# A pre-LN attention and SwiGLU block: where the feed-forward weights are summed and split

## The chip, the core and the metric

The kernel runs on one core of a Trainium2 chip. Five engines work side by side, each through its own instructions in order: TensorE (PE; its weight loads are listed as PEld), VectorE (DVE), ScalarE (ACT), GpSimd (POOL) and SyncE (SP), which issues nearly all DMA transfers here. They meet only at semaphores. The metric is device time of one execution in microseconds (us); lower is better.

## The reference

One transformer block on 2048 tokens of width 640, 32 heads of 20, a feed-forward width of 1728, all in f32:

```
x = A_x
h = x + attention(layernorm(x), A_wqkv, A_wo)       # softmax(q k^T / sqrt(20)) v, then @ wo
z = layernorm(h)
out = h + (silu(z @ w_gate) * (z @ w_up)) @ w_down
```

## The kernel before

**Precision.** Most products are made from a high part, rounded to the fast matmul format (fp32r), and a low part, the rest: `split` writes the high part on ScalarE (line 74) and the low one by a subtraction on another engine (line 75). A product of two split operands is three matmuls: high x high, high x low, low x high.

**Stages.** (1) Normalisation, q, k, v and a part of the row maxima, up to about 370 us. (2) Attention, to about 1545 us: 32 units (8 groups of four heads, 4 chunks of 512 queries) of 16 key tiles. One step is one key tile: four score matmuls (`scores`, line 796), four exponentials on ScalarE (802), four weighted sums of an earlier step (`weigh`, 806), and row maxima for later units (`max_one`, 175 and 181) spread by `ORDER`. When a unit's maxima are complete, `max_all` (line 185) reduces them on VectorE and copies and splits them on GpSimd (`both`, 192 and 193); two steps later `max_finish` transposes them on TensorE (200), copies them on ScalarE (202), and SP writes them into rows of the query tile by four transfers (207). After a unit, its sums go through DRAM to be spread over partitions (819, 829, 835), GpSimd multiplies (841) and SP stores (844). (3) The projection of the last chunks, to about 1590 us. (4) The feed-forward stage, to the end.

**The feed-forward stage.** The 1728 columns of gate and up are cut into 14 blocks (the last of 64 columns), and the 2048 tokens into two pairs of chunks. `elements` is the list of (pair, block), the half block first in each pair. Gate and up of a block are computed together by a scheme of seven products (`UNITS`: A11, S2, A12, S1, S3, A22, S4, made from sums and differences of quarters of the weights and of the tokens) and four products with the last 128 rows (K4). `blocks` runs the products, `plain` those of the half block. One product is one step (8 a block, 6 in the half block), and after each, `step` issues what belongs beside it: some of the 16 pieces of the product with `w_down` of the block before (`down`, line 1026 on TensorE and the addition 1031 on VectorE), and preparations. Accumulators are four banks `ps_a` for products and four `ps_b` for `down`.

**Weights before the change.** `Weights` (669) loads a block's raw columns on SP (678), lets GpSimd make the four sums (704 to 711), and splits seven units of 128 x 256 and the last rows on ScalarE and GpSimd (`unit`, `last`, through 74 and 75) into a ring of 8 unit tiles and one of 3 last tiles. `load_down` and `split_down` do the same for 128 rows of `w_down`. Each block is prepared during the block before, and so each is loaded, summed and split twice, once a pair. Only the half block and the first whole one are made within attention, by GpSimd alone (`weights_ahead`, 718 and 719), from step (NU - NC) * NT + 5 = 453 of 512 on.

**The second pair's tokens.** `late_tokens` (1156) normalises, transposes, splits and sums chunks 2 and 3 while the first pair runs: 15 small items (`soon`), then 21 (`late`) of which four token tiles take five each: two flips (five transposes, copies and splits), sums on GpSimd, two splits. Results go to DRAM (`z_d`, `t_d`) from the tiles `kept`, of which each shape has two buffers. `soon` is taken one a step from step 3 of the first whole block on, `late` one every third step. During the last block of the first pair and the half block of the second, `swap` (1236) loads them back over the first pair's tiles.

Of the kernel before, what the change touches and what calls it, by code (L numbers as in the profile page):

```python
# [43 lines left out]
def tile_block(ctx: ExitStack, tc: tile.TileContext, x, wqkv, wo, wg, wu, wd, out):  # L44
# [11 lines left out]
    t_d = [dram.tile([P, 2, 4, CH], F32R, name=f"t_d{i}") for i in range(2)]  # L56

# [600 lines left out]
    rings = {}  # L658

    def place(kind):  # L660

        if not rings:
            rings["unit"] = [stay.tile([P, 8, 2, 2, P], F32R, name="units", tag="first"), 8, 0]
            rings["last"] = [stay.tile([P, 3, 2, 2, P], F32R, name="lasts", tag="second"), 3, 0]
        ring = rings[kind]
        ring[2] += 1
        return ring[0][:, (ring[2] - 1) % ring[1]]

    class Weights:


        def __init__(self, f):
            self.f, self.units, self.ahead = f, {}, False

        def load_one(self, i):
            f, src = self.f, (wg, wu)[i]
            cs = slice(f * P, (f + 1) * P)
            nc.sync.dma_start(self.raw[i], src[:, cs].rearrange("(k p) n -> p k n", p=P))

        def load(self):  # L680
            f = self.f
            both = pd1.tile([P, 2, ND, P], F32, name="raw")
            self.raw = [both[:, 0], both[:, 1]]
            self.ends = both[:, :, ND - 1]
            if f < NF - 1:
                for i in range(2):
                    self.load_one(i)
            else:
                self.load_half()

        def load_half(self):
            for i, src in enumerate((wg, wu)):
                nc.sync.dma_start(
                    self.raw[0][:, :, i * LASTW : (i + 1) * LASTW],
                    src[:, self.f * P :].rearrange("(k p) n -> p k n", p=P),
                )

        def sums(self, part, pool, tag):
            g, u = self.raw
            t = pool.tile([P, 2, 2, P], F32, name="sums", tag=tag, bufs=2)  # L700
            tt = nc.gpsimd.tensor_tensor
            a, b = t[:, 0], t[:, 1]
            if part == 0:
                tt(out=a, in0=u[:, 0:2], in1=u[:, 2:4], op=ALU.add)
                tt(out=b, in0=a, in1=g[:, 0:2], op=ALU.subtract)
                self.sources = {
                    "A11": g[:, 0:2], "A12": g[:, 2:4], "A22": u[:, 2:4], "S1": a, "S2": b,
                }
            else:
                tt(out=a, in0=g[:, 0:2], in1=u[:, 0:2], op=ALU.subtract)  # L710
                tt(out=b, in0=g[:, 2:4], in1=self.sources["S2"], op=ALU.subtract)
                self.sources.update({"S3": a, "S4": b})

        def part(self, src, hi, lo):
            if not self.ahead:
                split(src, hi, lo, nc.gpsimd)
                return
            nc.gpsimd.tensor_copy(hi, src)
            nc.gpsimd.tensor_tensor(out=lo, in0=src, in1=hi.bitcast(F32), op=ALU.subtract)

        def unit(self, kind, where="unit"):
            if self.f == NF - 1:
                k = 0 if kind == "A11" else 2
                src = self.raw[0][:, k : k + 2]
            else:
                src = self.sources[kind]
            t = self.units[kind] = place(where)
            self.part(src, t[:, 0], t[:, 1])

        def last(self):  # L730
            t = self.units["K4"] = place("last")
            n = 2 if self.f < NF - 1 else 1
            if self.ahead:
                for i in range(n):
                    self.part(self.raw[i][:, ND - 1], t[:, 0, i], t[:, 1, i])
            else:
                self.part(self.ends[:, :n], t[:, 0, :n], t[:, 1, :n])

        def tasks(self):

            u = self.unit
            if self.f == NF - 1:
                return [
                    [self.load], [], [lambda: u("A11")], [lambda: u("A12")], [self.last],
                ]
            return [
                [self.load], [],
                [lambda: self.sums(0, pd1, "sums"), lambda: u("A11")],
                [lambda: self.sums(1, pd1, "sums"), lambda: u("S2")],
                [lambda: u("A12"), self.last], [lambda: u("S1")],  # L750
                [lambda: u("S3"), lambda: u("A22")], [lambda: u("S4")],
            ]

        def raw_tile(self):
            return pc.tile([P, ND, P], F32, name="raw", tag="o_t")

    def weights_ahead():

        half, whole = Weights(NF - 1), Weights(0)
        half.ahead = whole.ahead = True  # L760

        def load_half():
            half.raw = [half.raw_tile()]
            half.load_half()

        def load(i):
            if i == 0:
                whole.raw = []
            whole.raw.append(whole.raw_tile())
            whole.load_one(i)  # L770

        nothing = lambda: None

        def half_first():
            keep = rings["unit"][2]
            rings["unit"][2] = 7
            half.unit("A11")
            rings["unit"][2] = keep

        tasks = [load_half, lambda: load(0), nothing, half.last]  # L780
        tasks += [lambda: half.unit("A12", "last"), half_first, lambda: load(1), nothing, nothing]
        tasks += [lambda: whole.sums(0, pc, "z2"), lambda: whole.sums(1, pc, "z2")]
        tasks += [lambda k=k: whole.unit(k) for k in UNITS] + [whole.last]
        return half, whole, tasks
# [86 lines left out]
    half_block, first_block, preparing = weights_ahead()  # L871
    for u in range(NU):
# [4 lines left out]
        for kt in range(NT):  # L877
# [45 lines left out]
            if kt in (12, 13) and 0 <= k + kt - 12 < ND:  # L923
                load_wo(k + kt - 12)
# [67 lines left out]
    def load_down(f):  # L992
        raw = pd2.tile([P, D], F32, name="d_raw")
        if f < NF - 1:
            nc.sync.dma_start(raw, wd[f * P : (f + 1) * P, :])
        else:
            for i in range(2):
                nc.sync.dma_start(raw[i * LASTW : (i + 1) * LASTW, :], wd[f * P :, :])
        return raw

    def split_down(raw):
        hi = pd2.tile([P, D], F32R, name="d_hi", bufs=2)
        lo = pd2.tile([P, D], F32R, name="d_lo", bufs=2)
        split(raw, hi, lo, nc.gpsimd)
        return hi, lo

# [10 lines left out]
    def down(c, t, half, wts, y_hi, y_lo, final):  # L1017
        d_hi, d_lo = wts
        tt = c * TPC + t
        pairs = [(y_hi, d_hi), (y_hi, d_lo)]  # L1020
        if y_lo is not None:
            pairs.append((y_lo, d_hi))
        hs = slice(half * HALF, (half + 1) * HALF)
        ps = ps_b()
        for n, (a, b) in enumerate(pairs):
            nc.tensor.matmul(  # L1026
                ps[:, :HALF], a[:, t * P : (t + 1) * P], b[:, hs],
# [9 lines left out]
    def to_come(c, wts, y, final):  # L1037
        pending.extend(
            lambda t=t, half=half: down(c, t, half, wts, *y, final)
            for t in range(TPC) for half in range(2)  # L1040
        )
# [11 lines left out]
    def plain(w, step, done):  # L1053

        u = w.units
        for i, order in enumerate(("124", "142")):
            z, ps = z2_c[i], bank()
            for n, k in enumerate(order):
# [7 lines left out]
                if n == 2:  # L1066
                    done(i, gated(ps))
                step()

    def blocks(w, step, done):  # L1070

        u = w.units
        z0, z1 = z2_c[0], z2_c[1]
        add = lambda out, ps, x: nc.vector.tensor_tensor(out=out, in0=ps, in1=x, op=ALU.add)  # L1074
# [6 lines left out]
        products(ps, two_of(u["S2"]), two_of(t32, 2))  # L1081
# [3 lines left out]
        products(ps, two_of(u["A12"]), two_of(z0, 2), True, False)  # L1085
# [5 lines left out]
        products(ps, two_of(u["S1"]), two_of(t14))  # L1091
# [228 lines left out]
```

## Time and profile before

| what | value |
|---|---|
| median of 3 runs | 2134.91 us (2133.05 to 2136.81) |
| the profiled execution, its own time | 2131.16 us |
| its span in the profile | 2129.2 us |
| TensorE busy, of the span | 98% |
| VectorE / ScalarE / GpSimd busy | 83% / 64% / 28% |
| granted TensorE clock | 0.998 |
| DMA, mean | 81 GB/s |

In the rows below, "out<-in xcount" names a group of instructions by the tiles it writes and reads; "| busy, mean ns | idle <-releaser" gives its total time in us, the mean of one instruction in ns, and how long the engine stood idle right before these instructions, with what ended the wait. A timeline row is start and length in us, and in brackets the idle time before it. A windows row is start:end and length in us, then each engine's busy us with its instructions, the granted clock, the busy share of the 16 DMA engines, and GB/s. Matmuls overlap, so their mean is longer than their spacing. A row of DMA in the chain of waits is a transfer from its issue to its landing. `SPq` rows are the issue of transfers by SP.

### The profile page before, as it was taken

The numbers are of one execution on the slowest core, as the hardware profiler recorded it, in microseconds if no ns is written. First come the engines' busy times: TensorE is split into PE (matmuls) and PEld (weight loads), VectorE is DVE, ScalarE is ACT, GpSimd is POOL, SyncE is SP. The second block draws the span as 40 slices with busy tenths as digits, with TensorE's granted clock in tenths as the row PEclk, the third lists the DMA queues.
The fourth block names the chain that finished last, engine by engine and source line by source line (L and its number), as shares of the span: only waits on it lengthen the run. The fifth ranks groups of instructions, "written<-read, shape, count | busy, mean of one in ns | idle before, by whom it ended". The sixth has DMA issues, their size and how long they took to land.

```text
span 2129.2 us, 34742 instructions
## 1 busy us (share of the span) xinstructions
PE 2094.9 (98%) x12726; PEld 1222.6 (57%) x12726; DVE 1761.4 (83%) x2929; ACT 1358.6 (64%) x2722; POOL 586.3 (28%) x644
## 2 busy tenths in 40 slices
PE   7999999999999999999999999999999999999999
PEld 5766775333333333333333333345588888888888
DVE  6999996999999999999999999986368776666666
ACT  4222217999998999989998999986733433233322
POOL 5222212000000000000000011031147888576664
PEclk9999999999999999999999999999999999999999
DMA  7565432110211211102103122121132343732111
GB/s 243 185 178 174 153 108 82 56 52 19 78 29 41 66 37 56 47 24 63 44 20 80 27 60 78 41 68 35 51 102 75 107 120 89 220 107 56 44 56 68
DMA packets 165009, 172.42 MB, mean 81 GB/s; under 512 B 41112, under 2 KB 109208, under 8 KB 164840
## 3 DMA queue, kind: packets, MB, share of 16 engines
q1 hardware_dynamic: 151256, 143.99, 23.1%
q10 hardware_dynamic: 13584, 26.23, 4.0%
q8 instruction: 100, 1.64, 0.3%
q14 instruction: 69, 0.57, 0.1%
HBM read 121.93 MB, written 47.45 MB: 80 GB/s over the span
## 4 chain that ended last, share of the span: by engine, by line
PE 88%; DVE 5%; DMA 3%; POOL 1%; issue 1%; SPq 1%; ACT 1%; ACTq 0%; POOLq 0%; DVEq 0%
PE acc L806 24%; PE ps_max L175 15%; PE ps_one L796 14%; PE ps_a L956 14%; PE ps_b L1026 8%; PE ps_one L416 4%; DVE mx L169 3%; PE ps_one L450 2%; PE ps_wide L165 2%; PE ps_max L606 2%; PE ps_b L606 1%; DMA qk_d<-e 1%; DMA raw<-in_B_w_up 1%; DVE mx L181 1%; DMA o_t<-o_d 0%
## 5 line engine op out<-in xcount | busy, mean ns | idle before, releaser
L802 ACT ACTIVATE probs<-ps_one 128x512 f32<-128x512 f32 x2048 | 1045.0, 623 | 133.7 <-PE ps_one L796 128.3
L181 DVE TENSOR_REDUCE mx<-ps_max 128x1 f32<-128x512 f32 x1632 | 1021.2, 683 | 97.6 <-PE ps_max L175 50.1
L796 PE MATMUL ps_one<-q_stk,k_stk 62*128 62x512 f32 x2048 | 551.8, 422 | 1.8 <-DMA h<-in_A_x 1.1
L806 PE MATMUL acc<-probs,v_stk 128*32 128x512 f32 x4096 | 546.3, 605 | 0.2
L175 PE MATMUL ps_max<-k_stk,q_stk 60*128 60x512 f32 x1632 | 542.3, 460 | 2.2 <-DVE mx L181 1.5
L175 PEld LDWEIGHTS ps_max<-k_stk,q_stk 60*128 60x128 f32 x1632 | 231.1, 184 | 428.9 <-DVE mx L181 410.0
L796 PEld LDWEIGHTS ps_one<-q_stk,k_stk 62*128 62x128 f32 x2048 | 300.1, 186 | 82.0 <-ACT probs L802 52.7
L169 DVE TENSOR_REDUCE mx<-ps_wide 128x2 f32<-128x1024 f32 x208 | 240.5, 1216 | 13.2 <-PE ps_wide L165 12.6
L1074 DVE TENSOR_TENSOR tmp<-ps_a,tmp 128x512 f32<-128x512 f32 x208 | 141.2, 690 | 132.6 <-PE ps_a L956 126.6
L192 POOL CAST both<-neg 128x16 fp32r<-128x16 f32 x32 | 6.6, 206 | 788.3 <-DVE neg L188 396.7
L1031 DVE TENSOR_TENSOR h<-ps_b,h 128x320 f32<-128x320 f32 x448 | 197.2, 482 | 13.2 <-PE ps_b L1026 13.0
L806 PEld LDWEIGHTS acc<-probs,v_stk 128*32 128x32 f32 x4096 | 80.8, 108 | 160.9 <-issue 152.6
L956 PE MATMUL ps_a<-t,units 128*128 128x512 f32 x624 | 162.7, 396 | 0.0
L1026 PE MATMUL ps_b<-d_hi,y_hi 128*128 128x320 f32 x448 | 138.6, 310 | 0.7 <-DVE h L1031 0.7
L1026 PE MATMUL ps_b<-d_lo,y_hi 128*128 128x320 f32 x448 | 137.7, 308 | 1.1 <-POOL d_lo L75 1.1
L74 ACT ACTIVATE y_hi<-tmp 128x512 fp32r<-128x512 f32 (+1 forms) x56 | 35.3, 632 | 161.9 <-DVE tmp L1075 156.9
L956 PE MATMUL ps_a<-z,units 128*128 128x512 f32 x504 | 130.9, 394 | 0.0
L1026 PE MATMUL ps_b<-d_hi,y_lo 128*128 128x320 f32 x416 | 127.6, 307 | 3.0 <-POOL y_lo L75 3.0
L956 PEld LDWEIGHTS ps_a<-t,units 128*128 128x128 f32 x624 | 112.6, 188 | 18.7
L956 PEld LDWEIGHTS ps_a<-z,units 128*128 128x128 f32 x504 | 90.8, 187 | 15.3
L1088 ACT ACTIVATE tmp<-tmp 128x512 f32<-128x512 f32 x26 | 16.5, 633 | 126.4 <-DVE tmp L1074 126.4
L956 PE MATMUL ps_a<-z,lasts 128*128 128x512 f32 x336 | 95.3, 393 | 0.0
(152 smaller groups left out, 2181.4 us busy)
## 6 DMA issues: line engine op xcount, KB each, us to landing
raw<-qk_d SPq DMA_DIRECT2D x70, 160.0 KB
k_stk<-qk_d SPq DMA_DIRECT2D x64, 160.0 KB
q_stk<-qk_d SPq DMA_DIRECT2D x64, 160.0 KB
raw<-in_B_w_gate SPq DMA_DIRECT2D x26, 320.0 KB
raw<-in_B_w_up SPq DMA_DIRECT2D x26, 320.0 KB
d_raw<-in_B_w_down SPq DMA_DIRECT2D x26, 320.0 KB
rb<-r_d SPq DMA_DIRECT2D x32, 256.0 KB
qk_d<-e ACTq DMA_DIRECT2D x22, 320.0 KB
```

Of the source, the lines that this page charges most:

```text
L169: nc.vector.tensor_reduce(mx[:, :, pair, t, kc], ps, axis=AX.X, op=ALU.max)
L175: nc.tensor.matmul(ps, queries[u][rows, pair, t * P : (t + 1) * P], keys[u // NC][rows, pair, kc * CH : (kc + 1) * CH], start=True, stop=True,
L181: nc.vector.tensor_reduce(mxs[u][:, b, pair, t, kc : kc + 1], ps, axis=AX.X, op=ALU.max)
L416: nc.tensor.matmul(ps, w[:, k, m * P : (m + 1) * P], a[:, k, :], start=(n == 0 and k == 0), stop=(n == 2 and k == ND - 1),)
L606: nc.tensor.matmul(ps[:, :HALF], a[:, k, :], w[:, k, hs], start=(n == 0), stop=(n == 3 * ND - 1),)
L796: nc.tensor.matmul(ps, keys[u // NC][rows, p, kt * P : (kt + 1) * P], queries[u][rows, p, :], start=True, stop=True,)
L802: nc.scalar.activation(probs[p][:, b, :], ps, AF.Exp, scale=scale)
L806: nc.tensor.matmul(acc[32 * j : 32 * j + 32, :], values[u // NC][:, kt, j * VW : j * VW + 32], probs[j // 2][:, j % 2, :], start=(kt == 0) ...
L956: nc.tensor.matmul(ps, w[k][:, i], z[k][:, j], start=(first and m == 0), stop=(last and m == len(n) - 1),)
L1026: nc.tensor.matmul(ps[:, :HALF], a[:, t * P : (t + 1) * P], b[:, hs], start=(n == 0), stop=(n == len(pairs) - 1),)
L1031: nc.vector.tensor_tensor(out=h, in0=ps[:, :HALF], in1=h, op=ALU.add)
L1074: add = lambda out, ps, x: nc.vector.tensor_tensor(out=out, in0=ps, in1=x, op=ALU.add)
```

## The change

All feed-forward weights are prepared once, within attention, on GpSimd alone, and written to DRAM (`w_d`: per block eight places of 128 x 512, seven units and the last rows; `d_d`: per block two half rows of `w_down`, high and low). `prepare_weights` gives a list of 204 tasks: for each whole block load, a pause, two pairs of sums, seven units and the last rows; for the half block load, pause, two units and the last rows; for `w_down`, of two blocks at a time, load, pause and four half rows. Each task first issues the stores of the task before. Raw weights use the tiles `o_t`, sums `z2`, results `o_hi` and `o_lo`, two buffers each, which nothing else uses at that time. From unit 1 on, each step takes one task, but for key tiles 3 and 4 and for the step in which `max_all` was just issued.

The last stage no longer sums or splits weights. Three rings of tiles are filled by SP from DRAM, a unit, a last or a half row at a time: `Ring.fill` is called at the start of each step and issues loads into places that had been freed at the call before. The rings of 8 units and 3 lasts are first filled at step (NU - NC) * NT + 8, that of 4 half rows when the projection is done. Also, `soon` is now taken five a step from the first step on, `late` one every step, and the pieces of `down` beside the first whole block are spread as 0, 0, 3, 3, 3, 3, 2, 2.

```diff
+    w_d = [dram.tile([P, 8, 4 * P], F32R, name=f"w_d{f}") for f in range(NF)]
+    d_d = [dram.tile([P, 2, 2 * HALF], F32R, name=f"d_d{f}") for f in range(NF)]
...
-    class Weights:
...
-    def weights_ahead():
...
+    def prepare_weights():
+        stores, count = [], [0]
+        def store():
+            while stores:
+                dst, t = stores.pop(0)
+                nc.sync.dma_start(dst.bitcast(F32), t.bitcast(F32))
+        def staged(shape):
+            count[0] += 1
+            return pc.tile(shape, F32R, name="staged", tag=("o_hi", "o_lo")[count[0] % 2])
+        def part(src, hi, lo):
             nc.gpsimd.tensor_copy(hi, src)
             nc.gpsimd.tensor_tensor(out=lo, in0=src, in1=hi.bitcast(F32), op=ALU.subtract)
...
+            def unit(kind):
+                store()
+                t = staged([P, 2, 2, P])
+                part(src[kind], t[:, 0], t[:, 1])
+                stores.append((w_d[f][:, UNITS.index(kind)], t.rearrange("p i k n -> p (i k n)")))
...
+    class Ring:
+        def __init__(self, places, plan):
+            self.places, self.plan = places, plan
+            self.issued = self.taken = self.freed = self.before = 0
+        def fill(self):
+            while self.issued < min(len(self.plan), self.before + len(self.places)):
+                place = self.places[self.issued % len(self.places)]
+                dst, src = self.plan[self.issued](place)
+                nc.sync.dma_start(dst.bitcast(F32), src.bitcast(F32))
+                self.issued += 1
+            self.before = self.freed
...
                 max_all(a[0])
+                quiet[0] = now[0]
...
-                    if preparing and now[0] >= (NU - NC) * NT + 5:
+                    if preparing and u and kt not in (3, 4) and quiet[0] != now[0]:
                         preparing.pop(0)()
+                    if now[0] == (NU - NC) * NT + 8:
+                        unit_ring, last_ring = weight_rings()
+                        unit_ring.fill()
+                        last_ring.fill()
...
-    def load_down(f):
...
-    def split_down(raw):
...
+        def by_unit(ps, *args):
+            products(ps, two_of(unit_ring.take()), *args)
+            unit_ring.free()
...
-        products(ps, two_of(u["A11"]), two_of(z0))
+        by_unit(ps, two_of(z0))
...
+    halves = pd2.tile([P, 4, 2, HALF], F32R, name="halves")
+    down_ring = Ring(
...
+    down_ring.fill()
...
-            each = [0, 0, 0, 3, 3, 3, 3, 4]
+            each = [0, 0, 3, 3, 3, 3, 2, 2]
...
-            for t in tasks[n]:
-                t()
-            if n == 3:
-                dn["parts"] = split_down(dn["raw"])
+            for ring in (unit_ring, last_ring, down_ring):
+                ring.fill()
...
-            if soon and (e > 1 or n >= 3):
-                soon.pop(0)()
-            elif late and not soon and count[0] % 3 == 0:
+            if soon:
+                for _ in range(5):
+                    if soon:
+                        soon.pop(0)()
+            elif late:
                 late.pop(0)()
```

More of the change, by code (lines that the diff above doesn't have):

```diff
@@ L657, in tile_block @@
     UNITS = ("A11", "S2", "A12", "S1", "S3", "A22", "S4")
[L658 to L667, printed above, removed]
-    class Weights:
[L672 to L717, printed above, removed]
@@ L730, in last @@
[L730 to L752, printed above, removed]
@@ L754, in raw_tile, with nothing @@
-        def raw_tile(self):
-            return pc.tile([P, ND, P], F32, name="raw", tag="o_t")
-    def weights_ahead():
[L759 to L784, printed above, removed]
+        def nothing():
+            store()
@@ new lines, in rows, with load, half @@
+        def rows(fs):
+            raw = {}
+            def load():
+                store()
+                for f in fs:
+                    raw[f] = pc.tile([P, D], F32, name="raw", tag="o_t")
+                    if f < NF - 1:
+                        nc.sync.dma_start(raw[f], wd[f * P : (f + 1) * P, :])
+                    else:
+                        for i in range(2):
+                            nc.sync.dma_start(
+                                raw[f][i * LASTW : (i + 1) * LASTW, :], wd[f * P :, :]
+                            )
+            def half(f, i):
+                store()
+                t = staged([P, 2, HALF])
+                part(raw[f][:, i * HALF : (i + 1) * HALF], t[:, 0], t[:, 1])
+                stores.append((d_d[f][:, i], t.rearrange("p i n -> p (i n)")))
+            return [load, nothing] + [lambda f=f, i=i: half(f, i) for f in fs for i in range(2)]
@@ new lines, in prepare_weights, with take, free @@
+        tasks = []
+        for f in range(NF):
+            tasks += block(f)
+        for f in range(0, NF, 2):
+            tasks += rows((f, f + 1))
+        return tasks + [store]
+    class Ring:
[9 more added lines that the diff above has]
+            self.before = self.freed
+        def take(self):
+            assert self.taken < self.issued
+            self.taken += 1
+            return self.places[(self.taken - 1) % len(self.places)]
+        def free(self, n=1):
+            self.freed += n
@@ new lines, in tile_block, with weight_rings, unit, last @@
+    ELEMENTS = [(pair, f) for pair in range(2) for f in (NF - 1, *range(NF - 1))]
+    def weight_rings():
+        def unit(f, i):
+            return lambda t: (t.rearrange("p i k n -> p (i k n)"), w_d[f][:, i])
+        def last(f):
+            n = 2 if f < NF - 1 else 1
+            return lambda t: (
+                t[:, :, :n], w_d[f][:, 7].rearrange("p (i k n) -> p i k n", i=2, k=2)[:, :, :n]
+            )
+        units = stay.tile([P, 8, 2, 2, P], F32R, name="units", tag="first")
+        lasts = stay.tile([P, 3, 2, 2, P], F32R, name="lasts", tag="second")
+        plan = [
+            unit(f, i) for _, f in ELEMENTS for i in (range(7) if f < NF - 1 else (0, 2))
+        ]
+        return (
+            Ring([units[:, i] for i in range(8)], plan),
+            Ring([lasts[:, i] for i in range(3)], [last(f) for _, f in ELEMENTS]),
+        )
@@ L990, in quarter_sums @@
         ]
-    def load_down(f):
[L993 to L999, printed above, removed]
-    def split_down(raw):
[L1002 to L1005, printed above, removed]
     def parts(f, s):
@@ L1015, in parts, with down @@
         return y_hi, None
-    def down(c, t, half, wts, y_hi, y_lo, final):
-        d_hi, d_lo = wts
+    def down(c, t, half, d, y_hi, y_lo, final):
         tt = c * TPC + t
-        pairs = [(y_hi, d_hi), (y_hi, d_lo)]
+        pairs = [(y_hi, d[:, 0]), (y_hi, d[:, 1])]
         if y_lo is not None:
-            pairs.append((y_lo, d_hi))
+            pairs.append((y_lo, d[:, 0]))
         hs = slice(half * HALF, (half + 1) * HALF)
@@ L1051, in gated, with plain @@
         return s
-    def plain(w, step, done):
-        u = w.units
+    def plain(step, done):
+        u = {k: unit_ring.take() for k in ("A11", "A12")}
+        u["K4"] = last_ring.take()
         for i, order in enumerate(("124", "142")):
@@ L1117, in blocks @@
         step()
-    order = [NF - 1, *range(NF - 1)]
-    elements = [(pair, f) for pair in range(2) for f in order]
-    wts = {0: half_block, 1: first_block}
     two, three = ahead, projection(3, ps_b)
```

128 lines of the change are left out of this document (85 added, 43 removed).

## The prediction

> **What bounds the kernel now.** I read the page's busy times first, then the engines by stage, then TensorE's idle time in the last stage, then the places where it stands still.
>
> ```profile
> span 2129.2 us, 34742 instructions
> ...
> PE 2094.9 (98%) x12726; PEld 1222.6 (57%) x12726; DVE 1761.4 (83%) x2929; ACT 1358.6 (64%) x2722; POOL 586.3 (28%) x644
> ```
> ```profile
> core 0: us, PE busy (x) PEld busy (x) DVE busy (x) ACT busy (x) POOL busy (x), PEclk, DMA share, GB/s
> 480.00:1600.00 1120.00, 1114.89 (x7451) 484.09 (x7449) 964.89 (x1640) 959.31 (x1907) 110.33 (x142) 1.00 0.19 51
> ...
> 1900.00:2000.00 100.00, 100.00 (x525) 87.69 (x524) 68.37 (x134) 31.68 (x74) 67.56 (x78) 1.00 0.18 50
> ```
>
> TensorE is busy 99.5% of attention and all of a quiet stretch of the last stage. GpSimd has 110 us of work in 1120 us of attention and 68 in 100 us afterwards: it has room where the change puts the work, and it does not bound the stage the work is taken from. What the change can win there is TensorE's idle time, and for the stretch from 1545 us to the end that is nearly all in these rows:
>
> ```profile
> L1026 PE MATMUL ps_b<-d_hi,y_hi 128*128 128x320 f32 x448 | 138.6, 310 | 0.7 <-DVE h L1031 0.7
> L1026 PE MATMUL ps_b<-d_lo,y_hi 128*128 128x320 f32 x448 | 137.7, 308 | 1.1 <-POOL d_lo L75 1.1
> ...
> L1026 PE MATMUL ps_b<-d_hi,y_lo 128*128 128x320 f32 x416 | 127.6, 307 | 3.0 <-POOL y_lo L75 3.0
> ```
> ```profile
> 1609.28 0.38 PE L1026 MATMUL ps_b<-d_hi,y_hi 128*128 128x320 f32 x1 [0.47 <-DVE h L1031]
> ...
> 1611.29 0.42 PE L1026 MATMUL ps_b<-d_hi,y_lo 128*128 128x320 f32 x1 [1.48 <-POOL y_lo L75]
> ...
> 1865.55 0.42 PE L1026 MATMUL ps_b<-d_lo,y_hi 128*128 128x320 f32 x1 [1.13 <-POOL d_lo L75]
> ...
> 1884.67 0.41 PE L1026 MATMUL ps_b<-d_hi,y_lo 128*128 128x320 f32 x1 [1.50 <-POOL y_lo L75]
> ```
>
> Two places: the first block, and the change from the first pair of chunks to the second. Both times GpSimd is late because sums and splits of weights queue ahead of what TensorE wants. That is 0.7 + 1.1 + 3.0 = 4.8 us, and no more.
>
> **GpSimd's new work in attention.**
>
> ```profile
> L704 POOL TENSOR_TENSOR sums<-raw 128x256 f32<-128x256 f32 x26 | 19.1, 736 | 56.6 <-DMA raw<-in_B_w_up 56.6
> ...
> L719 POOL TENSOR_TENSOR units<-sums,units 128x256 fp32r<-128x256 f32 x4 | 2.9, 733 | 0.3
> ...
> L718 POOL CAST units<-sums 128x256 fp32r<-128x256 f32 x4 | 1.6, 395 | 0.0
> L719 POOL TENSOR_TENSOR lasts<-raw,lasts 128x128 fp32r<-128x128 f32 x3 | 1.4, 458 | 0.2
> L718 POOL CAST lasts<-raw 128x128 fp32r<-128x128 f32 x3 | 0.9, 290 | 15.3 <-PE acc L806 15.3
> ```
>
> A whole block is 4 sums at 0.74, 7 units at 0.40 + 0.73 and two lasts at 0.29 + 0.46: 3.0 + 7.9 + 1.5 = 12.4 us, times 13 is 161. The half block is 3 us. Down weights are 28 pieces of 320 columns, about 1.3 us each by scaling the unit: 36. Together 200 us. Tasks number 13 x 12 + 5 + 7 x 6 + 1 = 204, one a key tile; counted through the loop with its skips they run from step 16 to step 254 of 512.
>
> ```profile
> 706.56 2.48 SPq L819 DMA_DIRECT2D r<-o  x4
> ...
> 729.30 2.73 SPq L207 DMA_DIRECT2D q_stk<-m  x4
> ...
> 743.34 2.47 SPq L819 DMA_DIRECT2D r<-o  x4
> ```
>
> One unit of 16 steps is 743.34 - 706.56 = 36.8 us, a step 2.30. So GpSimd is 200/547 = 37% busy there. Does that slow the others? The old kernel already did such work once, inside attention:
>
> ```profile
> 1000.00:1040.00 40.00, 40.00 (x274) 15.29 (x273) 36.98 (x62) 36.21 (x73) 1.71 (x3) 1.00 0.19 45
> ...
> 1380.00:1414.00 34.00, 33.98 (x235) 13.40 (x239) 31.49 (x53) 31.05 (x63) 16.32 (x31) 1.00 0.22 52
> ```
>
> With GpSimd 48% busy, TensorE issued 235/34 = 6.91 matmuls a us against 274/40 = 6.85, VectorE 1.56 against 1.55. Cost: nothing; TensorE's own matmuls cover it.
>
> **SP's new work in attention.**
>
> ```profile
> 1792.96 0.52 SPq L678 DMA_DIRECT2D raw<-in_B_w_up  x1
> ```
>
> It issues 135 stores and 43 loads more there, at about 0.5 us each (the row of one of these loads) 89 us of 547. Loads are 13.4 MB and stores 37 MB, 50 MB in 547 us: 92 GB/s on top of the 51 above, far from what the last stage shows below. Each store waits for the task before it, and SP is in order: behind it stand the query loads, the softmax sums and, most urgent, the four transfers of a unit's row maxima (L207), without which the unit's scores cannot start.
>
> ```profile
> 729.00 0.27 ACT L202 ACTIVATE m<-ps_one 32x128 fp32r<-32x128 f32 x1
> ```
> ```profile
> 1555.59 1.98 DMA r_d<-r
> ```
>
> Copy, issue and landing are 0.27 + 2.73 + 1.98 = 5.0 us. Counted in the loop, the maxima are closed 4 steps before their unit at the tightest (unit 15, 9.2 us), 5 steps for units 7, 11 and 16; the slack is 4 us, and one late GpSimd task is 1.1. Within 0 and the rival below I take +0.5.
>
> **The last stage loads.** A block needs 7 units and a last of 256 KB and two half rows of 320 KB, 2.75 MB, in place of three raw loads of 320 KB, 0.98 MB. A block is 102 matmuls (7 units of 6, 4 last products of 3, 16 down pieces of 3); at 525 in 100 us that is 19.4 us. So 142 GB/s replace 50. The ring runs about six units ahead, some 14 us.
>
> ```profile
> 1590.86 2.91 DMA d_raw<-in_B_w_down
> ...
> 1851.05 8.47 DMA raw<-in_B_w_up
> ```
>
> Quiet landings of 3 us and even the worst, 8.5, lie inside 14: nothing. ScalarE and GpSimd lose the splits; neither bounds.
>
> ```profile
> 1590.00 1.56 PE L956 MATMUL ps_a<-z,units 128*128 128x512 f32 x6
> ...
> 1594.90 1.56 PE L956 MATMUL ps_a<-t,units 128*128 128x512 f32 x6
> ```
>
> The first half rows go into the space that the projection leaves, as `d_raw` did, when the products begin at 1590. Two of them land some 1 us later than the 2.91 of the row above, at about 1594.5; they are first used after three units and a last, 1594.9 by these rows: covered, just.
>
> **The second pair's tokens come three times faster** (an item a step, not every third).
>
> ```profile
> 1640.00:1660.00 20.00, 20.00 (x111) 17.70 (x110) 15.27 (x29) 8.56 (x20) 15.41 (x16) 1.00 0.39 115
> ...
> 1835.00:1845.00 10.00, 10.00 (x54) 8.74 (x53) 6.42 (x13) 2.07 (x5) 3.39 (x4) 1.00 0.97 355
> ```
> ```profile
> z_d<-kept SPq DMA_DIRECT2D x8, 512.0 KB
> t_d<-kept SPq DMA_DIRECT2D x8, 512.0 KB
> ...
> z_d<-kept SPq DMA_DIRECT2D x8, 128.0 KB
> ```
>
> Their stores cost 0.39 - 0.18 = 0.21 of the DMA engines for 115 - 50 = 65 GB/s, 310 GB/s at full share; reloads reach 355 at 0.97. A token tile stores 2.36 MB in five steps, now 12.1 us: 7.6 us of DMA, and 1.72 MB of weights another 4.8: 12.4 of 12.1 us, just full, for about 50 us. The Trainium skill (DMA: Bandwidth & Descriptors, Specifications) says transfers of 512 B already run at line rate. By that these stores, of 512 B runs, would take 6.6 us and the sum 11.4, not full; the rows say 310 rather than 355, so I keep 12.4.
>
> VectorE too has more to do at once:
>
> ```profile
> L1031 DVE TENSOR_TENSOR h<-ps_b,h 128x320 f32<-128x320 f32 x448 | 197.2, 482 | 13.2 <-PE ps_b L1026 13.0
> ...
> L1074 DVE TENSOR_TENSOR tmp<-ps_a,tmp 128x512 f32<-128x512 f32 x208 | 141.2, 690 | 132.6 <-PE ps_a L956 126.6 <-ACT tmp L1078 3.1 <-POOL y_lo L75 1.0
> ...
> L1172 DVE TENSOR_SCALAR z<-h,mvs,r_late 128x640 f32<-128x640 f32 x8 | 7.5, 941 | 0.0
> ```
>
> In a step with a flip it has an add (0.69), two or three down-adds (0.48) and an apply (0.94), 2.6 to 3.1 us, against 1.4 to 2.1 of product, 0.9 of down matmuls and the transposes. In the first block three steps of this follow the moments, so I charge 1 us of waiting there, and 1.5 for the rest, where ScalarE also waits for a `kept` buffer; bounds 0 and the rival below.
>
> **The reload between the pairs.** DMA is full there already. The weights add about 1.8 MB to the block in which the reload is issued, 5 us at 355 GB/s. The last reload (K1) is issued before 1848.7, and the lines show when it is used:
>
> ```profile
> 1843.53 5.05 SPq L1236 DMA_DIRECT2D z<-z_d  x3
> ```
> ```profile
> 1858.88 0.85 PE L956 MATMUL ps_a<-z,lasts 128*128 128x512 f32 x3
> ```
>
> If it took 8.5 us as the load behind it did, it landed by 1857.1; plus 5 is 1862.2, 3.3 us late. If 5, not late. I take +1.5 of 0 to 3.3.
>
> **Sum.** The profiled execution took 2131.16 us. 2131.16 - 4.8 + 0.5 + 1 + 1.5 + 1.5 = 2130.9. The median of the runs is 3.75 above that execution, so 2134.6.
>
> **Rivals.**
> (a) Nothing new waits. Then the 4.8 us stand: 2130.1, faster by 0.22%. For it: the row at 1835 shows TensorE at 10.00 of 10 us with DMA full. Against it: three new pressures at once. Chance with the cases a little short of it but over 0.2%: 0.22.
> (b) Slower: stores of the second pair's tokens hold the two `kept` buffers. The fourth buffer of a token tile is stored one step, 2.4 us, before its slot is wanted. If a store takes 8.5 us, as the load at 1851 did, ScalarE stands 6 us, two such places a tile, four tiles. ScalarE frees product banks and makes the silu, and TensorE has four banks, some 1.5 steps or 3.7 us; 2.4 us times 8 is 19: 2154. It decides from a store time of about 6 us. Chance 0.22, most of it at half the price.
> (c) Slower: row maxima come late because SP is held behind a raw load and a GpSimd wait. A hold of 8.5 us less the slack of 4.2, at the four tight units: 17 us, 2152. Against it: GpSimd runs ahead between two maxima. Chance 0.08.
> (d) The loads do not keep up and TensorE waits for units: 142 GB/s against 355 speaks against it; 50 us of full DMA at 5% over is 2.5 us, 2137. It counts with no change.
>
> **Chances and range.** A change of 0.2% (4.3 us) is about what a measurement tells from none. My forecast, within it, has 0.44 with (d); faster 0.24 ((a), and 0.02 for waits hidden in modelled matmul ends); slower 0.32 (b, c, and 0.02 for others). The range reaches from 2128.5, somewhat below (a), to 2148, half of (b); my forecast's own is 2130.6 to 2139.
>
> **What would show it.** Right: the attention span from 480 us keeps its length and 6.85 matmuls a us with GpSimd near 37%; no idle of L1026 behind GpSimd at the first block and at the change of pairs; the DMA share near 1 from 1600 to 1650; small waits of TensorE behind VectorE in that window. Wrong: TensorE or ScalarE waiting for L207's transfers at a unit's start (c); ScalarE held by `kept` for microseconds (b); matmuls released by `units` or `halves` loads (d); or a pace of attention below 6.8 matmuls a us, which would break the argument from 1380 us.

## The result and the profile after

The changed kernel takes 2144.0 us (median of 8 runs, 2139.47 to 2154.28) against 2135.23 us for the kernel before (8 runs, 2130.27 to 2136.81). The ratio is 1.0049 with an interval of 1.0031 to 1.0068: slower by about half a per cent, where 2134.6 and "no change" was forecast.

The profiled execution of the changed kernel took 2144.3 us. Its page and the windows that answer to those of before:

```profile
span 2142.5 us, 35011 instructions
...
PE 2100.7 (98%) x12726; PEld 1224.7 (57%) x12726; DVE 1758.3 (82%) x2929; ACT 1281.1 (60%) x2491; POOL 495.0 (23%) x633
```
```profile
480.00:1600.00 1120.00, 1107.75 (x7410) 475.20 (x7403) 959.61 (x1627) 958.93 (x1906) 248.00 (x393) 1.00 0.30 90
1900.00:2000.00 100.00, 100.00 (x522) 87.50 (x521) 67.49 (x133) 15.66 (x25) 13.04 (x10) 1.00 0.44 145
```

The work moved as the change says: in the quiet stretch of the last stage GpSimd falls from 68 to 13 us in 100 and ScalarE from 32 to 16, and GpSimd gains 138 us between 480 and 1600 us. But TensorE, which was busy for 1114.89 us of this window, is now busy for 1107.75, and issues 41 matmuls fewer.

To place the loss, the execution is cut at ScalarE's first and last copy of a unit's sums (`o<-acc`, line 816 before, 846 after) and at the last addition of a `down` product. Timeline rows of the kernel before:

```profile
377.46 0.63 ACT L816 ACTIVATE o<-acc 128x512 f32<-128x512 f32 x1
1544.93 0.60 ACT L816 ACTIVATE o<-acc 128x512 f32<-128x512 f32 x1 [0.52 <-issue]
2118.47 7.49 DVE L1031 TENSOR_TENSOR h<-ps_b,h 128x320 f32<-128x320 f32 x18
```

The same of the changed kernel:

```profile
380.64 0.63 ACT L846 ACTIVATE o<-acc 128x512 f32<-128x512 f32 x1
1559.12 0.60 ACT L846 ACTIVATE o<-acc 128x512 f32<-128x512 f32 x1 [0.52 <-issue]
2130.40 7.49 DVE L1052 TENSOR_TENSOR h<-ps_b,h 128x320 f32<-128x320 f32 x18
```

The last stage is counted to the start of the last addition, which is the end of its row less that addition's own 0.49 us.

| stretch, us | before | after | difference |
|---|---|---|---|
| to the first copy | 377.5 | 380.6 | +3.2 |
| attention, first copy to last | 1167.5 | 1178.5 | +11.0 |
| last copy to the last addition | 580.5 | 578.3 | -2.3 |
| the rest of the span | 3.7 | 5.1 | +1.4 |

The first stretch has the same code, and across the nine profiles of this study it lay between 374.7 and 384.2, so its 3 us are no effect of the change. The last row, 3.6 to 5.4 in the nine, was not followed up. The loss is in attention, the gain in the last stage, smaller than the 4.8 us there were to win.

**Attention.** From copy to copy, 28 of the 31 distances differ by less than 0.1 us from those of before. Three are longer, by 1.55, 6.10 and 3.59 us. TensorE stands still in each, as its timeline shows:

```profile
586.47 0.28 PE L202 MATMUL ps_one<-ident,both 128*32 128x128 f32 x1 [1.47 <-POOL both L195]
...
623.03 0.39 PE L202 MATMUL ps_one<-ident,both 128*32 128x128 f32 x1 [4.11 <-POOL both L195]
...
845.71 0.28 PE L202 MATMUL ps_one<-ident,both 128*32 128x128 f32 x1 [1.98 <-POOL both L195]
```

Each is the transpose of a unit's row maxima (`max_finish`), waiting for `both`, which GpSimd makes. At the second place the timelines of VectorE, GpSimd and SP read:

```profile
615.37 0.22 DVE L190 TENSOR_REDUCE neg<-mx 128x16 f32<-128x64 f32 x1
```
```profile
621.01 0.72 POOL L708 TENSOR_TENSOR sums<-raw 128x256 f32<-128x256 f32 x1 [21.20 <-DMA raw<-in_B_w_up]
621.81 0.72 POOL L709 TENSOR_TENSOR sums<-sums,raw 128x256 f32<-128x256 f32 x1
622.48 0.20 POOL L194 CAST both<-neg 128x16 fp32r<-128x16 f32 x1
```
```profile
610.74 0.57 SPq L865 DMA_DIRECT2D rb<-r_d  x1
611.36 0.47 SPq L669 DMA_DIRECT2D w_d<-staged  x1
611.89 0.42 SPq L696 DMA_DIRECT2D raw<-in_B_w_gate  x1
612.35 0.65 SPq L696 DMA_DIRECT2D raw<-in_B_w_up  x1
613.04 2.85 SPq L139 DMA_DIRECT2D q_stk<-qk_d  x4
```

The maxima were ready at 615.6, but the copy into `both` began at 622.48. GpSimd had done nothing for 21 us: the next instruction in its order was the first sum of a block whose raw weights, issued at 611.89 and 612.35, had not arrived, and the copy stood behind it. The other two places look the same. These three loads were issued 9.2, 8.7 and 7.2 us before their first use could start, most others 4.1 to 6.7. Why the three took longer was not tested; a late load alone does no harm, for in the run with four pauses (below) one took 9.2 us as well, to a first use at 473.14, and no transpose waited for it.

The second place cost 6.10 us for 4.11 of idle time. Windows of 2 us show what else happened (the column ahead of the DMA share is the granted clock):

```profile
618.00:620.00 2.00, 0.92 (x8) 0.01 (x3) 1.18 (x2) 1.09 (x3) 0.00 (x0) 1.00 0.78 166
620.00:622.00 2.00, 0.00 (x0) 0.00 (x0) 0.00 (x0) 0.00 (x0) 0.91 (x2) 0.67 0.44 130
622.00:624.00 2.00, 0.97 (x5) 0.65 (x7) 0.00 (x0) 0.27 (x1) 1.92 (x5) 0.50 0.04 10
624.00:626.00 2.00, 2.00 (x11) 0.81 (x11) 1.79 (x3) 1.39 (x3) 1.92 (x4) 0.50 0.02 4
626.00:628.00 2.00, 2.00 (x14) 0.68 (x7) 0.32 (x2) 0.77 (x3) 1.92 (x4) 0.63 0.28 103
628.00:630.00 2.00, 1.93 (x15) 0.44 (x11) 2.00 (x4) 2.00 (x5) 1.76 (x6) 1.00 0.59 202
```

From 620 to 621 even VectorE and ScalarE stand still, and GpSimd until its load is there. Then the clock is at half until about 627.5, 4.5 us after TensorE resumed: 2.2 us of work lost, near the 6.10 - 4.11 = 2.0 that were to be explained.

**The last stage.** Of the 4.8 us behind GpSimd and VectorE 0.5 are left, and new waits stand at the second pair's tokens:

```profile
1611.70 0.74 PE L1232 MATMUL ps_a<-ident,z 128*128 128x128 f32 x5 [0.73 <-DVE z L1216]
1643.23 0.33 PE L1232 MATMUL ps_a<-ident,z 128*128 128x128 f32 x1 [0.81 <-ACT zz L1237]
1643.73 0.96 PE L993 MATMUL ps_a<-z,lasts 128*128 128x512 f32 x3 [0.16 <-DVE kept L77]
1656.93 0.33 PE L1232 MATMUL ps_a<-ident,z 128*128 128x128 f32 x1 [0.35 <-ACT zz L1237]
1657.43 1.67 PE L993 MATMUL ps_a<-t,units 128*128 128x512 f32 x6 [0.17 <-DVE kept L77]
1669.69 0.42 PE L1047 MATMUL ps_b<-halves,y_lo 128*128 128x320 f32 x1 [0.27 <-POOL y_lo L77]
```

Together 2.5 us. The waits of the same stretch say that ScalarE stood behind the stores of `kept` (longest wait in the last column):

```profile
ACT kept L76 <- DMA t_d<-kept: 12.1, 5, 4.5
...
ACT kept L76 <- DMA z_d<-kept: 6.8, 3, 4.1
```

At the reload between the pairs TensorE does not wait at all:

```profile
1850.00:1860.00 10.00, 10.00 (x53) 8.75 (x52) 5.96 (x12) 0.63 (x1) 0.00 (x0) 1.00 1.01 386
1860.00:1870.00 10.00, 10.00 (x56) 8.92 (x55) 7.69 (x16) 1.90 (x3) 2.59 (x2) 1.00 1.03 400
```

### The profile page after: what moved, and what is told of

It reads as the page before. It is cut to its first block, busy times and chain, and to the rows that moved or that the text cites. A ratio compares the mean times of both kernels' runs of the same rounds, so it can differ in the third digit from the quotient of the medians.

```text
span 2142.5 us, 35011 instructions
## 1 busy us (share of the span) xinstructions
PE 2100.7 (98%) x12726; PEld 1224.7 (57%) x12726; DVE 1758.3 (82%) x2929; ACT 1281.1 (60%) x2491; POOL 495.0 (23%) x633
## 4 chain that ended last, share of the span: by engine, by line
PE 87%; DVE 6%; DMA 3%; POOL 2%; issue 2%; ACT 1%; SPq 0%; ACTq 0%; POOLq 0%; DVEq 0%
PE acc L836 23%; PE ps_a L993 14%; PE ps_max L177 14%; PE ps_one L826 14%; PE ps_b L1047 8%; PE ps_one L418 5%; DVE mx L171 3%; PE ps_one L452 2%; PE ps_wide L167 2%; PE ps_max L608 2%; PE ps_b L608 1%; DMA t_d<-kept 1%; DVE mx L183 1%; POOL zz L1249 0%; PE ps_one L386 0%
## 5 line engine op out<-in xcount | busy, mean ns | idle before, releaser
L1047 PE MATMUL ps_b<-halves,y_hi 128*128 128x320 f32 x896 | 197.6, 309 | 0.2 <-DVE h L1052 0.2
L1047 PEld LDWEIGHTS ps_b<-halves,y_hi 128*128 128x128 f32 x896 | 156.8, 188 | 20.7 <-DVE h L1052 2.0
L77 POOL TENSOR_TENSOR y_lo<-tmp,y_hi 128x512 fp32r<-128x512 f32 x52 | 67.9, 1305 | 386.1 <-PE ps_a L993 241.9
L1047 PE MATMUL ps_b<-halves,y_lo 128*128 128x320 f32 x416 | 127.5, 307 | 0.3 <-POOL y_lo L77 0.3
```

Of the source, the lines that this page charges most:

```text
L77: lo_engine.tensor_tensor(out=lo, in0=src, in1=hi.bitcast(F32), op=ALU.subtract)
L1047: nc.tensor.matmul(ps[:, :HALF], a[:, t * P : (t + 1) * P], b, start=(n == 0), stop=(n == len(pairs) - 1),)
```

## The experiments

Theory Q: the copy into `both` stands in GpSimd's order behind the first use of a raw load that has not landed. With one pause, counted through the loop, three units (numbered from 0) have such a first use queued at or just ahead of `max_all` with few steps between the load and the transposes: unit 7 with 5 steps, units 8 and 14 with 4; the next has 7. These are the three that stall. The rivals are named in each expectation. The experiments came in two groups, each beside its own runs of the kernel before (medians 2135.36 and 2134.77 us); unless something else is said, an experiment is the changed kernel with one edit. The ratios are estimated by themselves and differ a little from the quotients of the medians.

| experiment | median us | ratio to before, interval | attention us | last stage us |
|---|---|---|---|---|
| four pauses | 2132.56 | 0.9987 (0.9973 to 1.0002) | 1167.2 | 578.4 |
| old pace of the tokens | 2142.52 | 1.0030 (1.0014 to 1.0046) | 1177.9 | 575.5 |
| both of these | 2130.09 | 0.9972 (0.9955 to 0.9989) | 1167.3 | 575.1 |
| no pause | 2140.09 | 1.0017 (1.0001 to 1.0032) | 1174.1 | 579.6 |
| two pauses | 2134.0 | 0.9999 (0.9987 to 1.0010) | 1169.5 | 579.6 |
| `both` on VectorE | 2143.7 | 1.0052 (1.0037 to 1.0068) | 1177.2 | 578.5 |
| before, with the new pace | 2161.81 | 1.0126 (1.0099 to 1.0152) | 1171.9 | 604.0 |

**Four pauses.** Each raw load gets four steps instead of one before its first use.

```diff
-                [load, nothing, lambda: sums(0), lambda: sums(1)]
+                [load] + [nothing] * 4 + [lambda: sums(0), lambda: sums(1)]
```

The lists of the half block and of `w_down` get the same edit.

> Theory Q (queue): all that attention lost, 11.2 us in three places, is the row maxima's copy (both) standing in GpSimd's queue behind a task that waits for a raw load; with four pauses after each load, not one, no first use falls less than 10 steps ahead of a transpose of maxima that is queued behind it, so attention takes what it took before (1167.4 us from the first to the last row-sum copy, each unit within 0.1 us of before), TensorE has no idle behind both, and the time is 2144.0 - 11.2 = 2132.8 us. Theory T (traffic): SP and DMA, busier by 92 GB/s, hold the maxima's transfers; the pauses take no transfer away, so attention stays near 1178 us and the time near 2144.

All 31 distances are again those of before within 0.35 us, attention is 11.3 us shorter, and the median 11.4 below the changed kernel's. GpSimd's timeline at the place of the longest stall now has the copy as soon as VectorE delivers, and the sums after it:

```profile
612.10 0.20 POOL L194 CAST both<-neg 128x16 fp32r<-128x16 f32 x1 [8.31 <-DVE neg L190]
...
626.26 0.73 POOL L708 TENSOR_TENSOR sums<-raw 128x256 f32<-128x256 f32 x1 [7.99 <-DMA raw<-in_B_w_up]
```

GpSimd does the same work in attention as in the changed kernel, and the loss is gone: it was the order, not the amount.

**Old pace of the tokens.** `soon` and `late` are taken as before the change.

```diff
-            if soon:
-                for _ in range(5):
-                    if soon:
-                        soon.pop(0)()
-            elif late:
+            count[0] += 1
+            if soon and (e > 1 or n >= 3):
+                soon.pop(0)()
+            elif late and not soon and count[0] % 3 == 0:
                 late.pop(0)()
```

> Only the pace of the second pair's tokens is put back (one small item a step, a token item every third step). Theory C (crowding): the 2.5 us of TensorE idle between 1600 and 1670 us go, the last stage takes some 576 us from the last row-sum copy to the last down-addition instead of 578.3, and the time is 2141.5 us; attention keeps its three stalls (1178 us). Rival: DMA full of weight loads sets the idle whatever the pace; then it stays at 2 us or more and the time at 2144.

The three stalls stay (1.50, 4.17 and 1.78 us), the last stage falls by 2.8 us. One window of it, and the same of the changed kernel:

```profile
1600.00:1700.00 100.00, 100.00 (x533) 87.88 (x532) 73.70 (x158) 22.39 (x40) 25.27 (x22) 1.00 0.55 180
```
```profile
1600.00:1700.00 100.00, 97.52 (x516) 83.78 (x516) 74.76 (x155) 29.88 (x58) 47.13 (x43) 1.00 0.77 237
```

At the old pace TensorE is busy for all of it: the 2.5 us of waits came from the pace.

**Both of these.** Four pauses and the old pace together.

```diff
+                [load] + [nothing] * 4 + [lambda: sums(0), lambda: sums(1)]
...
+            elif late and not soon and count[0] % 3 == 0:
                 late.pop(0)()
```

> Both edits together: four pauses, old pace of tokens. Theories Q and C together: 2144.0 - 11.2 - 2.5 = 2130.3 us, about 5 us below the kernel before, which is the 4.8 us of idle behind GpSimd that the change could take away. If either falls, 2133 (only Q holds) or 2141 (only C holds).

The two effects add up. Attention has the length of before, the last stage is 5.4 us shorter, and the whole is faster than either kernel, by 0.28% of the one before. The groups of the two `down` products that waited 4.8 us in all before the change now read:

```profile
L1047 PE MATMUL ps_b<-halves,y_hi 128*128 128x320 f32 x896 | 197.2, 309 | 0.2 <-DVE h L1052 0.2
...
L1047 PE MATMUL ps_b<-halves,y_lo 128*128 128x320 f32 x416 | 127.4, 306 | 0.0
```

**No pause.** The first use follows the load in the next step that takes a task, which moves every later task too.

```diff
-                [load, nothing, lambda: sums(0), lambda: sums(1)]
+                [load] + [nothing] * 0 + [lambda: sums(0), lambda: sums(1)]
```

> No pause after a load: the first use follows one step later. Theory Q, from the places in the loop alone: only unit 14's maxima are closed 4 steps after a load with a first use ahead of them (worth 3.6 to 6.1 us), and unit 6's 6 steps after (0 to 1 us), in place of three; attention some 1172 us and the time about 2138, faster than with the pause. A rival for which a load simply needs its pause says slower: every one of 21 first uses waits longer, 2150 or more.

A shorter pause gives a smaller loss, which a theory of "too little time for the load" alone does not allow: one stall instead of three, at the unit that the count named.

```profile
829.76 0.45 POOL L676 CAST staged<-raw 128x320 fp32r<-128x320 f32 x1 [14.49 <-DMA raw<-in_B_w_down]
...
832.42 0.20 POOL L194 CAST both<-neg 128x16 fp32r<-128x16 f32 x1
```
```profile
832.97 0.39 PE L202 MATMUL ps_one<-ident,both 128*32 128x128 f32 x1 [2.86 <-POOL both L195]
```

That distance is 5.32 us longer than before for 2.86 of idle time. The last distance but one is 1.38 longer as well, without a wait for `both`. The same was seen with two pauses (1.62) and in the last experiment below (4.78). No edit is needed for it, since the last experiment has the code of the kernel before up to there. In each of the three the granted clock fell to half at that place, here:

```profile
1494.00:1498.00 4.00, 4.00 (x15) 1.81 (x15) 0.89 (x2) 3.38 (x8) 0.00 (x0) 0.57 0.65 200
```

4 us at 0.57 are 1.7 us of work lost. With two pauses the clock was at half for 3.4 us from 1500.3 on. In the last experiment it was at half for 6.8 us from 1497.4 on, worth 3.4, next to a stop of 2.77 us; the kernel before stops there for 1.08 and keeps a clock of 1.00.

**Two pauses.**

```diff
-                [load, nothing, lambda: sums(0), lambda: sums(1)]
+                [load] + [nothing] * 2 + [lambda: sums(0), lambda: sums(1)]
```

> The changed kernel with two pauses after each load in place of one (four in the earlier run, none in another). By Q the stall hangs on the number of steps from the step that issues a raw load to the transposes, where a first use of that load is queued ahead of the copy into `both`: 4, 4 and 5 steps gave the three waits with one pause. With two pauses the count gives one place with 5 steps (the sixth unit) and one with 6 (the sixteenth), the next 7 or more: at most one or two small waits of 0 to 1.5 us, the units 7, 8 and 14 as in the kernel before, attention 1167 to 1170, time 2133 to 2135. Rival (any raw load issued right behind the broadcast of rb holds the maxima, whatever stands on GpSimd): stalls of 2 to 4 us at other units as well, attention 1174 or more, about 2140.

The three stalled units are free again. Of the two places that the count gave, the one with 5 steps (unit 5) did not stall, the one with 6 (unit 15) did, a little:

```profile
883.06 0.28 PE L202 MATMUL ps_one<-ident,both 128*32 128x128 f32 x1 [0.54 <-POOL both L195]
```

So the count says where a stall can be, and its size hangs on what else lies on GpSimd there: at unit 15 two pieces of `w_down` and the product of line 871 with `rb` lay between the landing and the copy. The rival, that any raw load near the broadcast holds the maxima, does not hold.

**`both` on VectorE.** The loads and every weight task stay.

```diff
-        nc.gpsimd.tensor_copy(ends[u][:, 0], neg)
-        nc.gpsimd.tensor_tensor(
+        nc.vector.tensor_copy(ends[u][:, 0], neg)
+        nc.vector.tensor_tensor(
```

> The changed kernel with one edit: in the row maxima the copy and the subtraction that make `both` go from GpSimd to VectorE; loads, pauses, and every GpSimd weight task stay where they are. Theory Q (the copy stands in GpSimd's order behind a weight task that waits for its raw load): the three waits of 1.5, 4.1 and 2.0 us at the transposes go, since VectorE waits for no load; the three long units fall back, attention 1178.5 -> about 1167 us. What is added is 64 small operations of about 0.2 us on a VectorE that is busy 92 per cent of attention or less: 0 to 10 us. Time 2133 to 2140. Rival (SP or the raw load itself holds the rows r_d, rb or q_stk back, and GpSimd only shows it): the three units stay long, attention 1178 or more, time 2144 or more.

GpSimd waits as long for the same load as in the changed kernel, and in attention no engine waits for GpSimd:

```profile
618.35 0.73 POOL L708 TENSOR_TENSOR sums<-raw 128x256 f32<-128x256 f32 x1 [21.25 <-DMA raw<-in_B_w_up]
```
```profile
L202 PE MATMUL ps_one<-ident,both 128*32 128x128 f32 x32 | 9.1, 284 | 0.0
```

The three stalls are gone, so the queue on GpSimd was needed for them. The time is no better, though, and lies above what was expected: most distances are now 0.2 to 0.5 us longer, about what the two operations take on VectorE:

```profile
L194 DVE CAST both<-neg 128x16 fp32r<-128x16 f32 x32 | 6.7, 208 | 1.1
L195 DVE TENSOR_TENSOR both<-neg,both 128x16 fp32r<-128x16 f32 x32 | 5.8, 181 | 1.1
```

0.208 + 0.181 = 0.39 us for each unit, 31 times, is 12; attention grew by 9.8. So some four fifths of it came through, although VectorE is busy for only 940 of 1080 us there (480 to 1560). That these two operations are the whole of the growth fits the sizes, but no run shows it.

**Before, with the new pace.** The kernel before, its weights summed and split in the last stage as ever, with five small items a step and a token item in every step.

```diff
-            count[0] += 1
-            if soon and (e > 1 or n >= 3):
-                soon.pop(0)()
-            elif late and not soon and count[0] % 3 == 0:
+            if soon:
+                for _ in range(5):
+                    if soon:
+                        soon.pop(0)()
+            elif late:
                 late.pop(0)()
```

> The kernel before with only the crowded pace of the token items in the last stage (five small items a step, a token item every step); its weights stay summed and split in the last stage as before. If the crowding alone makes the idle of TensorE at 1600 to 1670 us (2.5 us in the changed kernel): the last stage grows from 580.6 by 2.5 us or more, since GpSimd and ScalarE also split weights there, waits of TensorE for VectorE, ScalarE or GpSimd appear between 1600 and 1670, and the time is 2137 to 2141. Rival (the DMA loads of the prepared weights are needed for it): last stage 580 to 581.5, time 2134 to 2136.

The direction is as expected, the size is not: 23.5 us in the last stage, where 2.5 or more and a time of 2141 at most had been expected. Its groups of TensorE that wait:

```profile
L1026 PE MATMUL ps_b<-d_hi,y_lo 128*128 128x320 f32 x416 | 128.3, 308 | 6.7 <-POOL y_lo L75 6.7
...
L1188 PE MATMUL ps_a<-ident,z 128*128 128x128 f32 x40 | 6.6, 284 | 10.2 <-ACT zz L1193 8.1 <-DVE z L1172 1.9 <-ACT tmp L1078 0.3
```
```profile
1600.00:1700.00 100.00, 83.29 (x408) 69.05 (x407) 62.33 (x128) 35.32 (x81) 78.26 (x83) 0.95 0.46 138
```

GpSimd is busy for 78 of these 100 us, the DMA engines for 46%. TensorE's idle time in the last stage grows from 6.7 to 22.6 us, which is 15.9 of the 23.5; the granted clock was also at half for 6.8 us from 1647.5 and for 3.4 us from 1685.1 on, worth another 5.1. So the pace makes TensorE wait without any load of prepared weights. The changed kernel has the same pace and waits 2.5 us; its GpSimd is busy for 47 of these 100 us, which fits, but the change differs in more than that from this experiment. How much of these 2.5 is due to a DMA share of 0.77 was not separated.

## Why the prediction was wrong

**The gain, -4.8.** This term was right, though its 4.8 us are not "nearly all" of TensorE's idle time from 1545 us on, which was 6.7: the other 1.9 stand in the projection, before the products begin. With both costs removed the last stage is 5.4 us shorter, and its `down` products wait for 0.2 us, a wait ahead of the very last products that the kernel before has too. TensorE's idle time in that stage fell by 4.1 us only; the other 1.3 were not followed up, and the rest of the span, 5.0 us in place of 3.7, took 1.2 back.

**GpSimd's work in attention, 0.** It was right as a statement about the amount: GpSimd is busy for 38% of the time from 380 to 960 us, where 37% was forecast, and 28 distances of 31 are unchanged. The argument from 1380 us did not cover order: there a wait of 3.3 us for a load ended at 1390.92, and the next copy into `both` came at 1410.13.

**SP and the row maxima, +0.5.** This is the step that failed: "the slack is 4 us, and one late GpSimd task is 1.1". It followed the maxima from VectorE's result on through ScalarE's copy, SP's four transfers and their landing, and left out that GpSimd copies and splits them first, a step that the description of the stages names, in the same order as the weight tasks. A late GpSimd task there is not 1.1 us of work but a whole wait for a load, up to 9 us after its issue. Measured: +11.0 in place of +0.5. The three long distances make 1.55 + 6.10 + 3.59 = 11.2, of which 1.47 + 4.11 + 1.98 = 7.6 us are idle time; the half clock (2.2 and 1.7 us by the windows) accounts for the other 3.7 within half a us. The slack counted was also that of the transfers, at the start of the unit that uses the maxima; the transposes stand in TensorE's order two steps after `max_all` and stop it at once.

**The crowded tokens, +1 and +1.5.** The sum was right: 2.5 us by the trace, 2.8 by the run with the old pace. The mechanism was right in part. VectorE comes first (0.73 us at 1611.70), and the waits of 0.81 and 0.16 at 1643 us follow waits of ScalarE, 4.12 and 1.92 us, for stores of `kept`. But ahead of the 0.35 and 0.17 at 1657 us ScalarE had waited 4.64 us for GpSimd's sums of the tokens. And the DMA engines were not "just full, for about 50 us": their share from 1600 to 1650 was 0.76, and 1.01 only in single stretches such as 1630 to 1640, at 304 GB/s, near the 310 that the prediction had taken for these stores.

**The reload, +1.5.** This term was too large: the reload cost nothing at a DMA share above 1. The estimate let the weights push the last reload back; in the trace its products did not wait. Only the run with the old pace shows a wait of that kind, 0.70 us.

**The rivals.** (a), nothing new waits, 2130.1: this is what the run with both edits shows, 2130.09. That the two agree to 0.01 us is luck, since the runs of that kernel lie between 2124.82 and 2133.98. (b), ScalarE behind the stores of `kept`: the waits are there, 12.1 and 6.8 us, but they reach TensorE with 2.5 us at most, not 19. (c) had the right ingredients, late maxima behind a raw load and a wait of GpSimd, but it held SP and charged the wrong units (7, 11, 15 and 16; they were 7, 8 and 14) because it looked at the transfers' slack. It had 0.08. The wrong engine in the queue made the likeliest way to lose look remote. (d): no product waited for `units` or `halves`.

The parts account for the time: 2144.0 less the 11.3 us of attention that four pauses return, and less the 2.8 of the pace, is 2129.9; the run with both edits took 2130.09.

## What to carry to other kernels

Work that "fills idle time" on an in-order engine must not wait there ahead of something urgent: an instruction that waits for a load closes the engine to the small, urgent operations behind it, and the price is the load's landing, not the instruction's length. The waiting itself is harmless: with four pauses GpSimd still waited up to 12.7 us for a load, at no cost. Put such first uses further from their load than the slowest landing seen, or right behind the urgent operation (which was not tried here), and count the steps from load to urgent operation for every pass of the loop, since a few bad alignments (three of 32 here) carry the whole loss. When a result is followed from engine to engine for its slack, start at the first instruction that touches it, and list what else stands on that engine.

## What the runs showed of the hardware

**The clock after a stop.** The granted clock fell to half at stalls of TensorE behind `both` of 4.11, 2.86 and 1.98 us, and with the old pace of the tokens at 4.17 and 1.78; it stayed at 1.00 after 1.47 and 1.50. For the stall of 1.98 the windows of the changed kernel read:

```profile
844.00:846.00 2.00, 0.29 (x3) 0.18 (x3) 0.00 (x0) 0.00 (x0) 1.84 (x5) 0.99 0.56 133
846.00:848.00 2.00, 2.00 (x11) 1.16 (x15) 1.25 (x2) 1.09 (x3) 1.84 (x4) 0.50 0.80 272
848.00:850.00 2.00, 2.00 (x12) 0.47 (x14) 0.73 (x2) 1.24 (x3) 1.97 (x3) 0.66 0.57 142
850.00:852.00 2.00, 1.91 (x17) 0.66 (x13) 1.86 (x4) 1.83 (x4) 0.87 (x1) 1.00 0.61 216
```

Half clock lasts until about 849.4, 3.7 us after TensorE resumed at 845.71, worth 1.7 us; the distance grew by 3.59 - 1.98 = 1.6 more than the idle time. The Trainium skill (TensorE: Matmul & The Clock Gate, Part 1) says that an idle window of about 3.4 us drops the clock to half and that about 3.4 us of sustained work restore it. The restoring agrees roughly, with 3.4 to 6.2 us from TensorE's resuming after these five stalls; the drop came after less, 1.78 us, so here the measured stops decide. A stall that brought half clock cost 1.4 to 1.9 times its idle time. The length of a stop alone does not say whether the clock falls: half clock also followed a stop of 0.90 us (no pause, from 1494.6 on), and did not follow one of 1.50. What the traces' clock records do show is a fixed grid: within a run, any two starts of half clock lie a whole number of 3.413 us apart (620.67 and 845.95 in the changed kernel, 66 of them), and each half clock lasted 3.41 or 6.83 us, but for the one at the end of the program.

**Full DMA without a loss.** TensorE was busy for 10.00 of 10 us while the DMA engines moved 386 and 400 GB/s at a share above 1. With the old pace one product did wait there, 0.70 us for the reload, at a share of 1.02 (1860 to 1875).
